# Polysketch attention and a top-2 router in one kernel: the head's order, TensorE's sketch sums and the last stores changed

## The chip, the core and the metric

The kernel runs on one core of a Trainium2 chip. Its engines are TensorE (PE; PEld is its weight load), VectorE (DVE), ScalarE (ACT), GpSimd (POOL) and SyncE (SP), which here only issues transfers. Each engine works through its own instructions in order and waits on semaphores. The metric is the device time of one execution in microseconds (us); less is better. Before the change the median of three runs is 347.21 us (346.69 to 347.39).

## What is computed

Inputs: q, k, v of 4 batches, 4 heads, 1088 tokens, head size 32; two sketch matrices S1, S2 (8 x 32, float64, read as words and split by the kernel); gate and noise weights (128 x 8), noise (4352 x 8), and w1 (128 x 1024), w2 (1024 x 128) of 8 experts.

```python
def phi(x):
    a = np.einsum('rd,bhsd->bhsr', S1, x)
    b = np.einsum('rd,bhsd->bhsr', S2, x)
    return np.einsum('bhsi,bhsj->bhsij', a, b).reshape(*x.shape[:-1], r * r)
q_p, k_p = (phi(q), phi(k))
kv = np.einsum('bhsf,bhsd->bhfd', k_p, v)
z = np.sum(k_p, axis=2)
num = np.einsum('bhsf,bhfd->bhsd', q_p, kv)
den = np.einsum('bhsf,bhf->bhs', q_p, z)[..., None] + 1e-06
# x = num / den, heads side by side: 4352 tokens of 128
noisy_logits = x @ w_gate + np.log1p(np.exp(x @ w_noise)) * noise
# the two best experts of each token, softmax weights top2_w over the two
h = np.maximum(x[mask] @ w1[e], 0.0)
out[mask] += top2_w[mask, k, None] * (h @ w2[e])
```

## The kernel before, in words

**Planner.** Nothing is issued in the order of the source. `add` gives a `Plan` a job: engine or choice of engines, a cost in us, the tiles it reads and writes, and `prio`. `Plan.order` is a list scheduler: among the jobs that can start within 0.3 us of the earliest it takes the least `prio`. So a changed cost or priority can move instructions on every engine, far from where it stands. Tile tags have a number of buffers; a job that opens a tile waits for the oldest user.

**Head, batch 0.** `decode_job` makes the sketch matrix `sk` on VectorE and TensorE, in a high and a low part (index c). `turned` transposes loaded keys (`kT`) or queries (`qT`) on VectorE. `features` multiplies them by `sk`, both parts side by side in a bank (L606); it evicts the low part to `lo` (ACT or DVE, L322), adds it to the high part on VectorE (`ab`, L614) and forms the products (`phk`, `phq`, L628). Keys of batch 0 come in tiles 0-1, 2-5, 6-7 and the half tile 8 (`C`). `keys_values` copies the values into `vaug`, sums keys x values on TensorE (L669), evicts them (`kvT`), folds in identity and gate weights (`wg`, L690), and evicts that as `kvw` in two halves. `queries` transposes the query sketches (L717, `pT`), makes numerators, denominators and gate logits in one matmul (L728), then on VectorE divisors and gates (`den`, `lh`, `lg`), on ACT or VectorE `x`. Two early sketches, of the rest of the queries of batch 0 and of the first keys of batch 1, have `early` set: they use the `acc` banks and stand between numerators and router. While TensorE would be idle in the head, `idle` puts warming matmuls of zeros there (`hp<-zb`).

**Router.** `router` computes noisy logits (VectorE, ACT, GpSimd), picks two experts, counts tokens per expert by matmuls of the mask `mk` with a triangle (L934, L937), works out each row's place (`to`), weighs the tokens (`xg`), and scatters them with GpSimd's indirect transfers to `xs` in DRAM (L809). The first half of batch 0 is router 0, the rest of it router 1, then batches 1 to 3. `clear` fills `xs` from `pad` ahead of the scatters.

**Experts.** `block` handles 128 or 256 rows of an expert: rows to `bT`, two matmul layers (L1108 into `hp`, relu on ACT, L1123 into `acc`), `y`, and a scatter into `pairs`. Blocks 0 to 3 take their rows by a one-hot matmul (`o`, L1047, L1050, L1054 and `turn`, L1060), blocks 4 to 7 fetch `xb` by GpSimd and turn it on TensorE (L1084), later ones fetch by SP and turn it on VectorE (L1096). The one-hot of the last of four token columns is made by two ACT operations.

**GpSimd's head.** Constants in a list by priority: `pads` (`pad`), `limits` (`reach`, `capt`), `numbers` (`pid`), the copies of the noise, and a choice of the value copies.

**End.** `sums` adds the two pairs of each token and stores them. For the last tiles of batch 3 the last two experts' results are not scattered but put in place by one-hot matmuls in `totals` (L1255) and added (L1186). The pieces are tiles 4-5, the half tile, tiles 6-7, all stored by ACT.

Of the kernel before, what the change touches and what calls it, by code (L numbers as in the profile page):

```python
# [174 lines left out]
def kernel(  # L175
# [27 lines left out]
    C = 8  # L203
# [58 lines left out]
    tag("lo", 2, [P, 4, 2 * R * H])  # L262
    tag("ab", 2, [P, 4 * H, 2, R])
# [54 lines left out]
    def copy(e, o, i):  # L318
        if e == "POOL":
            G.tensor_copy(o, i)  # L320
        else:
            paces.append(A.copy(o, i) if e == "ACT" else V.tensor_copy(o, i))  # L322

# [111 lines left out]
    def pool_job(cost, prio, emit, w, r=()):  # L435
        add("POOL", cost, lambda e: emit(), r=r, w=w, prio=prio)

    def constants():
# [51 lines left out]
        pool_job(1.2, 13, pads, ["pad"])  # L490
# [6 lines left out]
        pool_job(0.5, 14, lambda: limits(0, 1), [("limits", 0)], ["base"])  # L497
# [11 lines left out]
        pool_job(2.4, 15, numbers, ["pid"])  # L509
        pool_job(3.0, 16, lambda: limits(1, NW + 1), [("limits", 1)], ["base"])  # L510
# [84 lines left out]
    def features(jobs, prio, after=(), first=None, early=None):  # L595
# [7 lines left out]
        def emit(e):  # L603
            for i, (xT, t, _) in enumerate(jobs):
                lhsT = xT.t[:, P * t:min(P * t + P, S)]
                T.matmul(ps.t[rows, 2 * W * i:2 * W * i + 2 * W], lhsT=lhsT,  # L606
                         rhs=sk[:].rearrange("p c h x -> p (c h x)"), start=True, stop=True)
        last = (add if early is None else plan.add)("PE", n * mm(128), emit, lat=0.15, r=["sk"] + [(xT, t) for xT, t, _ in jobs],
                   w=[ps], prio=prio if first is None else first, touch=[dst for _, _, dst in jobs], after=after if early is None else (early,))
        lo, ab = new("lo"), new("ab")  # L610
        gone = [] if early is None else [onehot["pos"], onehot["gm"]]
        x4 = lambda: ps.t[rows, 0:2 * W * n].rearrange("p (i c y) -> p i c y", i=n, c=2)
        add(EV, either(W * n), lambda e: copy(e, lo.t[rows, 0:n, :], x4()[:, :, 1, :]), r=[ps] + gone, w=[lo], prio=prio)
        add("DVE", vec(W * n), lambda e: V.tensor_tensor(  # L614
            out=ab.t[rows, 0:n * H, :, :].rearrange("p (i h) w r -> p i (h w r)", h=H),
            in0=x4()[:, :, 0, :], in1=lo.t[rows, 0:n, :], op=ALU.add), r=[ps, lo], w=[ab], prio=prio if early is None else 12.95 if jobs[0][2] is kv_of[0][1] else 13.2)
# [20 lines left out]
    behind_gates = []  # L637

    def keys_values(b, prio, head=False, after=(), early=None):
        kT, qT, pk, pq, va = new("kT"), new("qT"), new("phk"), new("phq"), new("vaug")  # L640
        kld, qld, vld = klds[b], qlds[b], vlds[b]
        for h in range(H):
            add(("ACT", "POOL") if head else "ACT", {"ACT": act(256), "POOL": 0.4} if head else act(256), lambda e, h=h: copy(e, va.t[:, 0:C, h, 0:DH], vld.t[:, h, 0:C, :]),
                r=["ones_v"] + [(vld, l) for l in range(4)], w=[(va, h)], prio=prio + 2.2, after=hold)
        add("ACT", act(128), lambda e: A.copy(va.t[0:HB, C, :, 0:DH], vld.t[0:HB, :, C, :]),
            r=["ones_v", (vld, 4), (vld, 5)], w=[(va, H)], prio=prio + (2.9 if head else 2.2), after=hold)
        for i, (c0, c1) in enumerate(((0, 2), (2, 6), (6, 8)) if head else ((0, 4), (4, 8))):
            if early is not None and i == 0:
                turned(kT, kld, c0, c1, 22, True)
                features([(kT, t, pk) for t in range(c0, c1)], prio + i + 1, after, 21.5, early)  # L650
                continue
            freed.append(turned(kT, kld, c0, c1, prio + i))
            features([(kT, t, pk) for t in range(c0, c1)], prio + i + 1, after)
        freed.append(turned(kT, kld, 8, 9, prio + 1))
# [38 lines left out]
        for l in range(2):  # L693
            add(EV, either(98), lambda e, l=l: copy(
                e, kvw.t[64 * l:64 * l + 64, :, YW * l:YW * l + YW],
                ps.t[64 * l:64 * l + 64, 0:2 * YW].rearrange("p (a y) -> p a y", a=2)),
                r=[ps, "kvw0"], w=[(kvw, l)], prio=prio + 3)
        turned(qT, qld, 4, 8, prio + 5)
        if head:
            def rest(early):  # L700
                behind_first.append(features([(qT, C, pq)], prio + 26, (), 913))
                features([(qT, t, pq) for t in range(4, 8)], prio + 26, (), prio + 11, early)
# [71 lines left out]
    APART = "rows of other waves, or of other tokens"  # L774
# [41 lines left out]
    def router(b, t0, n, w, x, lg, prio):  # L816
# [28 lines left out]
        actf(0.25, lambda: A.activation(out=t3("sp"), in_=t3("u"), func=AF.Ln, bias=1.0), ["u"], ["sp"])  # L845
# [136 lines left out]
        indexed = dve(0.2 + 2 * vec(16 * n), index, ["first", "row"], ["f2", "at", "to"], late)  # L982
# [492 lines left out]
```

## Time and profile before

| what | us |
|---|---|
| median of 3 runs | 347.21 |
| profiled execution, its own time | 347.08 |
| its span in the trace | 345.1 |
| TensorE busy | 336.2 |
| first expert matmul starts | 27.47 |
| last matmul of TensorE starts its group (L1255) | 337.50 |
| last sum on VectorE starts | 339.25 |
| last store's issue starts, on ACT | 341.04 |

The span is counted from the first instruction to the last; the run's time has about 2 us more around it. In a timeline each line gives start, duration, engine, source line, operation, the tile written <- the tiles read, shapes, the number of instructions merged into the line, and in brackets the idle time of the engine ahead of it and what ended that. A float32 matmul appears as two passes. In the chain of waits each piece is what the end of the execution depended on at that time. "SPq" and "ACTq" are an engine's sequencer issuing a transfer.

### The profile page before, as it was taken

What the parts mean: (1) busy time and instruction counts of PE and PEld (TensorE: products, weight loads), DVE (VectorE), ACT (ScalarE), POOL (GpSimd) and SP (SyncE); (2) the same over time, 40 slices, a digit from 0 to 9 for tenths busy, and PEclk for the clock granted to TensorE, in tenths of its full rate; (3) what the DMA queues carried; (4) which work ended last, traced back from release to release, by engine and by line L of the source; (5) the groups of instructions that cost most, each with busy time, mean ns of one, the idle gap of its engine ahead of it and who ended that gap; (6) DMA issues with size and microseconds to landing.
All of it is one profiled execution on the core that took longest, in us unless ns stands there. A gap on an engine that the chain in (4) does not pass through costs nothing.

```text
span 345.1 us, 7493 instructions
## 1 busy us (share of the span) xinstructions
PE 336.2 (97%) x2585; PEld 313.9 (91%) x2586; DVE 146.4 (42%) x547; ACT 136.4 (40%) x305; POOL 232.1 (67%) x385
## 2 busy tenths in 40 slices
PE   8999999999999999999999999999999999999992
PEld 3859999999999999999999999999999999999992
DVE  5889794877636688555862000020102000112101
ACT  2357542543531445323334333433334333434430
POOL 8854868896899857898968889878334433354410
PEclk9999999999999999999999999999999999999997
DMA  7999839144571376511353213365125211114421
GB/s 217 327 346 268 288 63 356 60 116 114 139 221 39 62 187 133 138 40 39 74 74 71 54 43 54 69 184 120 37 36 185 67 32 27 29 32 166 147 77 39
DMA packets 68922, 41.17 MB, mean 119 GB/s; under 512 B 49877, under 2 KB 61078, under 8 KB 68880
## 3 DMA queue, kind: packets, MB, share of 16 engines
q1 hardware_dynamic: 63360, 30.93, 35.1%
q0 software_dynamic: 4704, 9.15, 8.2%
q10 hardware_dynamic: 816, 0.58, 0.6%
q8 instruction: 21, 0.34, 0.4%
q14 instruction: 21, 0.17, 0.2%
HBM read 24.18 MB, written 16.65 MB: 118 GB/s over the span
## 4 chain that ended last, share of the span: by engine, by line
PE 95%; DVE 2%; ACT 1%; issue 1%; POOL 0%; DVEq 0%; ACTq 0%; POOLq 0%
PE acc L1123 37%; PE hp L1108 37%; PE bank L606 5%; PE bank L728 4%; PE bank L669 4%; PE bank L717 2%; PE hp L1435 1%; PE acc L669 1%; PE bank L1255 1%; PE turn L1060 1%; PE bank L690 0%; ACT o L1050 0%; PE bank L937 0%; DVE lg L747 0%; ACT o L1047 0%
## 5 line engine op out<-in xcount | busy, mean ns | idle before, releaser
L1123 PEld LDWEIGHTS acc<-w2s,h 128*128 128x128 f32 x1152 | 145.8, 192 | 4.6
L1123 PE MATMUL acc<-w2s,h 128*128 128x128 f32 x1152 | 149.8, 275 | 0.0
L1108 PE MATMUL hp<-bT,w1s 128*128 128x128 f32 (+1 forms) x768 | 147.3, 328 | 0.2 <-ACT bT L322 0.2
L1116 ACT ACTIVATE h<-hp 128x512 f32<-128x512 f32 x144 | 86.0, 597 | 123.2 <-PE hp L1108 122.9
L1108 PEld LDWEIGHTS hp<-bT,w1s 128*128 128x128 f32 x768 | 111.6, 191 | 6.4 <-ACT h L1116 0.5
L809 POOL DMA_INDIRECT pairs<-y,ix x66 | 65.1, 986 | 66.1 <-ACT y L322 55.9
L809 POOL DMA_INDIRECT xs<-xg,to x72 | 73.0, 1014 | 19.2 <-issue 9.1
L808 POOL MEMSET zb<- 128x400 bf16 (+1 forms) x142 | 63.1, 444 | 0.2 <-PE hp L1435 0.2
L1096 DVE STREAM_TRANSPOSE bT<-xb 128x256 f32<-128x256 f32 (+1 forms) x40 | 15.6, 390 | 101.9 <-PE hp L1108 89.8
L322 ACT COPY y<-acc 128x128 f32<-128x128 f32 (+1 forms) x48 | 15.3, 320 | 28.1 <-PE acc L1123 27.6
L1179 DVE TENSOR_TENSOR o<-pr 128x512 f32<-128x512 f32 (+2 forms) x13 | 6.7, 525 | 36.1 <-DMA pr<-pairs 36.1
L728 PE MATMUL bank<-kvw,pT 128*128 128x98 f32 x144 | 18.2, 274 | 0.0
L728 PEld LDWEIGHTS bank<-kvw,pT 128*128 128x128 f32 x144 | 17.4, 192 | 0.6 <-DVE kvw L322 0.3
L669 PE MATMUL bank<-phk,vaug 128*128 128x128 f32 (+1 forms) x108 | 13.1, 277 | 0.0
L322 ACT COPY lo<-bank 128x256 f32<-128x256 f32 (+3 forms) x20 | 6.5, 328 | 16.5 <-PE bank L606 16.5
L322 ACT COPY pT<-bank 128x512 f32<-128x512 f32 (+1 forms) x16 | 8.8, 559 | 10.6 <-PE bank L717 9.1
L669 PEld LDWEIGHTS bank<-phk,vaug 128*128 128x128 f32 (+1 forms) x108 | 12.5, 191 | 0.4
L614 DVE TENSOR_TENSOR ab<-bank,lo 128x256 f32<-128x256 f32 (+3 forms) x20 | 7.2, 360 | 12.5 <-ACT lo L322 12.4
L628 DVE TENSOR_TENSOR phk<-ab 128x512 f32<-128x512 f32 (+1 forms) x20 | 12.2, 629 | 0.4
L628 DVE TENSOR_TENSOR phq<-ab 128x512 f32<-128x512 f32 (+1 forms) x20 | 11.8, 628 | 0.2
L991 DVE TENSOR_TENSOR xg<-x,g 128x512 f32<-128x512 f32 (+1 forms) x16 | 11.2, 750 | 0.0
L1435 PE MATMUL hp<-zb 128*128 128x512 bf16 x29 | 9.5, 463 | 1.6 <-DVE zb L439 1.3
(177 smaller groups left out, 243.7 us busy)
## 6 DMA issues: line engine op xcount, KB each, us to landing
xs<-pad SPq DMA_DIRECT2D x9, 516.0 KB
w1s<-in_moe_w_dram SPq DMA_DIRECT2D x8, 512.0 KB
w2s<-in_moe_w_dram SPq DMA_DIRECT2D x8, 512.0 KB
pr<-pairs SPq DMA_DIRECT2D x7, 512.0 KB
xb<-xs SPq DMA_DIRECT2D x96, 32.0 KB
kq<-in_k_dram SPq DMA_DIRECT2D x4, 544.0 KB
kq<-in_q_dram SPq DMA_DIRECT2D x4, 544.0 KB
vld<-in_v_dram SPq DMA_DIRECT2D x14, 128.0 KB
```

The source lines that it names most:

```text
L322: paces.append(A.copy(o, i) if e == "ACT" else V.tensor_copy(o, i))
L606: T.matmul(ps.t[rows, 2 * W * i:2 * W * i + 2 * W], lhsT=lhsT, rhs=sk[:].rearrange("p c h x -> p (c h x)"), start=True, stop=True)
L628: V.tensor_tensor(out=jobs[i][2].t[rows, jobs[i][1]:jobs[m - 1][1] + 1, :, :].rearrange("p c h (i j) -> p (c h) i j", i=R), in0=factors(i, ...
L669: T.matmul(kvp.t[:, P * a:P * a + P], lhsT=va.t[0:K, t, hs, :].rearrange("p h d -> p (h d)"), rhs=pk.t[0:K, t, hs, :].rearrange("p h f -> ...
L728: T.matmul(ps2.t[:, c0:c0 + 2 * YW], lhsT=pT.t[:, P * (2 * i + a):P * (2 * i + a) + P], rhs=kvw.t[:, a, :], start=True, stop=True)
L808: G.memset(zb[:, 0:FIRST_SPACER if kind == "first" else SPACER], 0.0)
L809: ins = G.indirect_dma_start(**kw)
L1096: add("DVE", vec(P * n), lambda _: V.transpose(bT.t[:, 0:P * n], flat()), r=[xb], w=[bT], prio=TOP + u)
L1108: T.matmul(hp.t[:, P * n * i:P * n * (i + 1)], lhsT=w1s[:, e, P * (js * g + i):P * (js * g + i + 1)], rhs=bT.t[:, 0:P * n], start=True, st ...
L1116: paces.append(A.activation(out=h.t[:], in_=hp.t[:], func=AF.Relu))
L1123: T.matmul(acc.t[:, D * c:D * c + D], lhsT=h.t[:, P * (n * i + c):P * (n * i + c + 1)], rhs=w2s[:, e, j, :], start=(j == 0 and c == 0), st ...
L1435: ins = T.matmul(warm()[:], lhsT=zb[:, 0:P], rhs=zb[:], start=True, stop=True)
```

## The change

- Buffers: `lo` is gone, `ab` has four buffers; the low part is evicted into `ab` and the sum made in place.
- Head order: `kT` of tiles 0-1 is turned at priority -51 (ahead of `sk`, -50), the next ones at 0.5 and 0.9, the half tile at 1.9. The first keys of batch 1 are turned after both halves of `kvw`.
- `summed`: the two early sketches are made by two matmuls of 64 columns per tile that accumulate in the bank; ACT evicts the sum in one copy, behind the router's logarithm.
- `kvw` of the head: one half on ACT, one on VectorE, declared to have no dependency on each other.
- GpSimd: page numbers (`numbers`), `pads` and the first limits behind the value copies, in that order; the other limits one by one, the last ones behind the first router's row indices.
- One-hots: block 0 has all four columns on VectorE; the ACT costs of the others are 0.45 for the planner.
- End: one store for tiles 4-7 by ACT, the half tile's by SP ahead of it; loads of these tiles (and of tiles 0-3) in two; the half tile's matmuls first.

As built, the order of instructions differs from before in these places that bear on time. On SP the keys of batch 1 and the weights of experts 1 and 2 stand ahead of the first two clears (before, three clears stood ahead of these weights). On GpSimd the second router's gate step (`g`, 128x5) stands ahead of the four fetches of `xb` and not behind them. On VectorE the copies `starts` and `over` stand between `c` and `noisy` of the first router. On TensorE there are fewer warming matmuls, and sketches, numerators and blocks 2 to 20 are interleaved differently.

```diff
+    tag("ab", 4, [P, 4 * H, 2, R])
...
     def pool_job(cost, prio, emit, w, r=()):
-        add("POOL", cost, lambda e: emit(), r=r, w=w, prio=prio)
+        job = add("POOL", cost, lambda e: emit(), r=r, w=w, prio=prio)
+        if 11 < prio < 11.5:
+            behind_values.append(job)
+        if prio == 17:
+            behind_choices.append(job)
...
-        pool_job(1.2, 13, pads, ["pad"])
+        pool_job(1.2, 11.45, pads, ["pad"])
-        pool_job(0.5, 14, lambda: limits(0, 1), [("limits", 0)], ["base"])
+        pool_job(0.5, 11.47, lambda: limits(0, 1), [("limits", 0)], ["base"])
-        pool_job(2.4, 15, numbers, ["pid"])
-        pool_job(3.0, 16, lambda: limits(1, NW + 1), [("limits", 1)], ["base"])
+        pool_job(2.4, 11.4, numbers, ["pid"])
+        for w in range(1, NW + 1):
+            pool_job(0.5 if w < NW else 0.3, 16 if w < 4 else 17, lambda w=w: limits(w, w + 1), [("limits", 1)], ["base"])
...
+                if summed:
+                    for c in range(2):
+                        T.matmul(ps.t[rows, W * i:W * i + W], lhsT=lhsT, rhs=sk[:, c, :, :].rearrange("p h x -> p (h x)"),
+                                 start=(c == 0), stop=(c == 1))
+                    continue
...
-        lo, ab = new("lo"), new("ab")
+        ab = new("ab")
+        if summed:
+            add("ACT", act(W * n), lambda e: copy(e, ab.t[rows, 0:n * H, :, :].rearrange("p x w r -> p (x w r)"), ps.t[rows, 0:W * n]),
+                r=[ps], w=[ab], prio=prio if early is None else 12, after=() if early is None else (onehot["sp"],))
+        else:
+            add(EV, either(W * n), lambda e: copy(e, flat(), x4()[:, :, 1, :]), r=[ps], w=[ab], prio=prio)
+            add("DVE", vec(W * n), lambda e: V.tensor_tensor(out=flat(), in0=x4()[:, :, 0, :], in1=flat(), op=ALU.add), r=[ps], w=[ab],
+                prio=prio)
...
-                turned(kT, kld, c0, c1, 22, True)
-                features([(kT, t, pk) for t in range(c0, c1)], prio + i + 1, after, 21.5, early)
+                turned(kT, kld, c0, c1, 22, True).deps.update(folded_first)
+                features([(kT, t, pk) for t in range(c0, c1)], prio + i + 1, after, 21.5, early, True)
-            freed.append(turned(kT, kld, c0, c1, prio + i))
+            freed.append(turned(kT, kld, c0, c1, (-51, 0.5, 0.9)[i] if head else prio + i))
...
+                if head:
+                    apart(ins, "kvw")
+                    wrote(ins, "kvw")
+            done = add(("ACT", "DVE")[l] if head else EV, 0.25 if head else either(98), half, r=[ps, "kvw0"], w=[(kvw, l)], prio=prio + 3)
...
-                if c == 3:
+                if c == 3 and u:
...
+            n = 2 if b == B - 1 and c == 4 else c
+            for d in range(0, c, n):
...
-        for k, cols in enumerate(((0, 1), (4,), (2, 3))):
+        for k, cols in enumerate(((4,), (0, 1), (2, 3))):
...
-    pieces = part_of(B - 1, [(4, 2), (6, 2)], True)
-    sums(B - 1, [pieces[0], pieces[2], pieces[1]], NW, 902, ("ACT",))
+    pieces = part_of(B - 1, [(4, 4)], True)
+    sums(B - 1, [pieces[1], pieces[0]], NW, 902, ("SP", "ACT"))
```

## The prediction

> **What bounds the kernel now.** I read the page's engine shares first, then the table by stage, then the chain of waits for the head, then the timelines of single engines where the change acts.
>
> ```profile
> PE 336.2 (97%) x2585; PEld 313.9 (91%) x2586; DVE 146.4 (42%) x547; ACT 136.4 (40%) x305; POOL 232.1 (67%) x385
> ```
> ```profile
> 27.47:47.73 20.26, 20.26 (x179) 19.95 (x180) 17.24 (x76) 11.64 (x32) 14.64 (x21) 1.00 0.81 226
> 47.73:70.00 22.27, 22.27 (x205) 21.66 (x203) 15.38 (x50) 8.29 (x20) 18.85 (x28) 1.00 0.53 173
> 70.00:150.00 80.00, 79.76 (x676) 77.12 (x675) 54.02 (x203) 32.96 (x77) 65.66 (x95) 1.00 0.51 126
> 150.00:320.00 170.00, 170.00 (x1217) 160.63 (x1216) 35.92 (x131) 65.95 (x124) 109.46 (x157) 1.00 0.30 73
> ```
> The columns after the stretch are its length, then the busy time of PE, weight loads, DVE, ACT and POOL. From 27.47 us on TensorE has no gap worth naming (0.24 us in 70 to 150). Time can be won only ahead of 27.47, where the expert work begins, and after TensorE's last matmul; anywhere else it can only be lost. The head's chain:
>
> ```profile
> 9.50 0.60 PE bank L606 x4
> 10.10 1.79 PE acc L669 x16
> 11.89 0.89 PE bank L606 x8
> 12.78 2.42 PE acc L669 x20
> 15.21 0.59 PE bank L717 x4
> ...
> 16.90 1.15 PE bank L728 x8
> ...
> 26.99 0.26 ACT lo L322
> 27.25 0.17 ACT bT L322
> 27.43 0.04 issue
> 27.47 2.05 PE hp L1108 x16
> ```
> From 9.50 to 15.21 TensorE is unbroken, and at the end two ACT copies in a row hold the first expert matmul: one evicts an early sketch, the next bT. The tail:
>
> ```profile
> 339.25 0.42 DVE L1186 TENSOR_TENSOR o<-o,bank 128x256 f32<-128x256 f32 x1 [0.36 <-PE bank L1255]
> ```
> ```profile
> 338.70 0.65 ACTq L338 DMA_DIRECT2D out_dram<-o  x1
> ```
> ```profile
> 339.45 1.50 ACTq L338 DMA_DIRECT2D out_dram<-o  x1
> ```
> ```profile
> 341.04 0.70 ACTq L338 DMA_DIRECT2D out_dram<-o  x1
> ```
> The last sum is ready at 339.67, but its store is issued at 341.04, because ACT is still issuing the half tile's.
>
> **What the Trainium skill says.** "TensorE: Matmul & The Clock Gate", section "LDWEIGHTS": a weight load takes its columns over 1.2, whatever else, thus 107 ns for 128 columns. The trace agrees: passes of 128 and of 98 columns both come every 0.11 us (1.79 us for 16, 1.76 for 16). "DMA: Bandwidth & Descriptors", "Anatomy of one DMA": about 2.0 us of a DMA are fixed. Here GpSimd waits 1.97 us after its last scatter. Same page, "Issuing engines are not separate DMA queues": a second issuing engine saves only issue time; here that is just what the tail lacks. "GPSIMD Engine Reference", specifications: GpSimd shares its SBUF interface with VectorE, so times of GpSimd vary; its two value copies took 0.66 and 0.40 us (the tile view).
>
> **The change part by part.** Times are of the profiled execution before.
>
> 1. First keys turned before the sketch. VectorE is idle from 5.55 to 6.15, waiting for TensorE, then does sk and the 0.36 us turn in a row; TensorE starts at 6.85. The trace's landing records put the keys' last piece at 5.93, so the turn fills only part of the gap: turn 5.95 to 6.31, sk to 6.62, TensorE at 6.66, a gain of 0.19. Tiles 6 and 7 are also turned before the first sum, so their sketches follow the others at once instead of at 9.50. With ACT's copy at 7.40 the sums and products run some 0.35 us earlier, the last small turn by 8.85, and TensorE is through its key sketches at 9.1. The 10.10 row can then start when the values are copied. GpSimd's two copies began at 8.52, behind the pads (7.33 to 8.51); now four small limits stand there, 0.89 us by the rows at 17.25 to 18.14, so copies from 8.3 to 9.3. Start 9.35 instead of 10.10: 0.75 earlier. Later products (10.9, 11.85, 12.65 for tiles 5, 7, 8) stay ahead of TensorE, so its end moves from 15.20 to 14.45. If GpSimd's small ones take longer, as one at 11.88 did with 0.64, it is 9.7 and 0.4. I take 0.7.
>
> 2. kvw halves on two engines. ACT's half starts at 16.32, VectorE's at 16.58 behind it, TensorE at 16.90. Declared apart, both run at 16.32: 0.26 less. Numerators at 15.95.
>
> 3. Keys of batch 1 turned after both halves, before the small query turn: from about 15.9 on VectorE. In before they landed at 17.05 by the landing records, after a 516 KB clear (15.79); now they take its place, at about 15.8. Turn to 16.6, small turn to 16.85, the divisors due at 17.1. No cost; each us that the keys come after 16.1 would stand on the path.
>
> 4. Copies of starts and over move between c and noisy: two small VectorE instructions, 0.08 us apart at 17.04: plus 0.12.
>
> 5. Early sketches summed by TensorE: 16 matmuls of 64 columns for 8 of 128, two passes each, so 32 passes of 0.11, not 16: 1.78 us more on TensorE from 17.8, to 21.4. Counts are due at 23.8. It replaces warming matmuls: nothing. ACT's two copies of 0.37 stand after the logarithm, the second at 21.4 and done at 21.8; the exponent behind it is due at 22.5: nothing. Were 64 columns dearer, at 0.15 a pass, it would be 0.3. Two 0.42 sums leave VectorE.
>
> 6. First one-hot wholly on VectorE, sketches' copies no longer ahead of bT. pos at 24.90 moves by 0.7 + 0.26 - 0.12 = 0.84 to 24.06. Four one-hots of 0.27 (1.62 for six) end at 25.4, the gathers at 25.8, ACT has done its pair by 25.35, bT 25.9, first expert matmul 26.2. Against 27.47: 1.25 us in all for the head.
>
> 7. GpSimd and SP. Page numbers and pads now follow the values: pads ready at 15.0 instead of 8.5, noise copies 15.5 to 17.8 (before 17.04), first needed at 20.6. The first two clears stand behind the weights of experts 1 and 2, so about 24.5 by the 3 us a pair takes; the first scatter needs them at 28.5. SP's queue keeps the weights moving: w1, w2 earlier, batch 1's values some 1.5 us earlier. Nothing on the path.
>
> 8. Scatters and the first fetches. VectorE reaches row at 26.2 (27.62 before), so scatters start at 28.5 (29.88) and end at 41.05 (42.45); landed 43.0. Now the second gate step stands before the four fetches on GpSimd, an added wait: behind it are the fetches, for which TensorE waits in order. It needs ACT's exponent, 45.61 before, 4.9 after the last numerators (40.67). In TensorE's new order these are done after 56 passes of experts and gathers and 38 more of the second router, 10.5 us after 26.2, so at 36.7; VectorE then has two rounds of divisors and gates of 1.05 before the 4.9 counted from the last round's end, less its own 1.1: the exponent at 42.6 to 42.8, the fetch at 43.3, landed 2.57 later (44.41 to 46.98 by the landing records), 45.9. TensorE asks for it at 26.2 + 20.26 - 0.44 (four sketch passes moved behind it) = 46.0. Cost nothing, 0.3 if any of this slips; before, there was 0.9 of slack (46.98 against 47.88).
>
> 9. Order of TensorE, VectorE and ACT from 28 to 100 differs because the planner sorts anew. Counts of matmuls after the start are equal, and I find no operand that is late by more than 0.2 through the first 20 us. Bounds: a gain of 0.2 (the gap in 70 to 150), a loss of 1.
>
> 10. Tail. The last tiles' matmuls keep their ten passes, the last sum still ends at 339.67. One store of 256 KB on ACT is issued at 339.72 instead of 341.04: 1.32 less. It moves twice the bytes with longer lines; 128 KB took about 0.6 us in the DMA view, so 0 to 0.6 more, I take 0.35. SP's half tile goes at 338.3, ahead. Net 0.95 (0.6 to 1.3). Splitting the loads adds VectorE instructions of 0.43 where it idles 10 us.
>
> Sum: 1.25 + 0.95 = 2.2 us. Span 345.1 becomes 342.9; the profiled execution took 347.08, so 344.9; the median of 347.21 is 0.13 above it, so 345.0.
>
> **Rivals.**
> A. The fetches hold TensorE. The head is shorter but block 4 waits at 46.0 for rows, a transfer chain that GpSimd's scatters pace at 1.57 us each. For: only 0.1 us of slack left. Against: the scatters start 1.4 earlier too. With scatters starting 0.6 later than I have it, 0.5 to 0.9 is lost: 345.8.
> B. The head does not move: value copies or keys of batch 1 late, so steps 1 and 3 give nothing; only 2, 6 and the tail remain, 0.26 - 0.12 + 0.41 + 0.95 = 1.5: 345.7. For: GpSimd's slow row at 11.88. Against: landing of a 516 KB clear at 15.79.
> C. Slower: the gate step on GpSimd. If the second router's exponent comes at 46.1 rather than 42.8 us, the fetch lands at 49.2 and TensorE stands 3.2 us at 46.0: 345.0 + 3.2 = 348.2. It decides from about 45.8 on (2.2 + 0.7 us lost). For: the exponent was at 45.61 before. Against: its numerators come 1.5 us earlier in TensorE's new order, besides the head's 1.25.
> D. The change is a wash: a few small stalls of step 9 eat the head, the one store is no faster: 347.2.
>
> **How the numbers follow.** What can be told from no change is 0.2%, 0.7 us: 346.5 to 347.9. Forecast 0.55, A 0.15, B 0.13, C 0.10, D 0.07. Faster 0.83, same 0.07, slower 0.10. The range runs from 344.1 (value copies at best, store at 1.3, the gap in 70 to 150 closed) to 346.9, leaving out C and about half of D.
>
> **What would show it.** TensorE's first expert matmul at 26.2 plus or minus 0.4, numerators near 16.0, VectorE's keys of batch 1 without a DMA wait, the transposes of block 4 with an idle time under 0.3, busy shares of 100% from 30 to 320, and one ACT store issued within 0.1 of the last sum. Wrong would be a first expert matmul after 27, TensorE waiting on xb, or more than 4.8 us from the store's issue to the span's end (4.06 before).

## The result, and the profile after

The changed kernel took 349.58 us (median of 8, 348.48 to 349.92), the kernel before beside it 347.03: a ratio of 1.0062, 95% interval 1.004 to 1.0083. The forecast was 345.0. Measured again in two other sets of runs (E5, E16 below), the same kernel took 347.70 and 347.71 us, ratios 1.0026 (1.0017 to 1.0034) and 1.0023 (1.0008 to 1.0039). So it is slower in all three; about 1.0 us of it comes back each time, and 1.5 us more belongs to the first measurement alone.

The profiled execution of the first measurement took 349.88 us, with a span of 348.2. Its table by stage, columns as before (stretch, length, then busy PE, weight loads, DVE, ACT, POOL):

```profile
27.47:47.73 20.26, 19.01 (x173) 18.67 (x171) 16.04 (x69) 10.21 (x27) 14.40 (x19) 1.00 0.76 228
47.73:70.00 22.27, 21.37 (x189) 20.62 (x190) 13.53 (x42) 7.75 (x20) 19.10 (x29) 1.00 0.59 185
70.00:150.00 80.00, 79.22 (x664) 75.73 (x664) 53.51 (x207) 31.70 (x76) 64.04 (x94) 1.00 0.52 125
150.00:320.00 170.00, 170.00 (x1215) 160.33 (x1214) 36.18 (x131) 66.54 (x125) 111.08 (x158) 1.00 0.31 69
```

TensorE was unbroken in all four stretches but for 0.24 us; now it stands still for 1.25, 0.90 and 0.78 us of the first three. Its timeline at the places that count:

```profile
26.32 0.38 PE L1135 MATMUL hp<-bT,w1s 128*128 128x128 f32 x1
```
```profile
43.55 0.71 PE L1150 MATMUL acc<-w2s,h 128*128 128x128 f32 x4 [1.04 <-ACT h L1143]
```
```profile
48.63 0.33 PE L1111 MATMUL turn<-ident,xb 128*128 128x128 f32 x1 [1.12 <-DMA xb<-xs]
```

The first expert matmul starts 1.15 us earlier than before (27.47), and then TensorE waits 1.04 us for ACT and 1.12 us for fetched rows. The chain of waits in this part (start, length, what):

```profile
31.71 3.24 POOL xs L833
...
41.38 0.97 POOL xs L833
42.35 3.25 issue
...
45.65 0.06 POOL g L968
...
46.47 2.12 DMA xb<-xs
48.59 0.04 issue
48.63 0.33 PE turn L1111
```

It runs over GpSimd: a scatter of 3.24 us, then the gate step `g`, then the fetch. Before, none of the first router's scatters was over 1.40 us, the gate step stood behind the fetches, and TensorE did not wait for the rows (GpSimd's and TensorE's timelines of before):

```profile
33.27 1.36 POOL L809 DMA_INDIRECT xs<-xg,to  x1 [0.17 <-issue]
34.63 0.34 POOL L808 MEMSET zb<- 128x280 bf16 x1
35.15 1.40 POOL L809 DMA_INDIRECT xs<-xg,to  x1 [0.17 <-issue]
...
44.41 2.22 POOL L338 DMA_DIRECT2D xb<-xs  x4 [1.97 <-DMA xs<-xg,to]
```
```profile
47.88 0.31 PE L1084 MATMUL turn<-ident,xb 128*128 128x128 f32 x1
```

So the fetch left at 44.41 before and at 46.47 now, while TensorE asks for the rows earlier than before. ACT's timeline says why the gate step came at 45.65:

```profile
39.13 0.37 ACT L321 COPY ab<-bank 128x256 f32<-128x256 f32 x1 [2.12 <-PE bank L618]
42.11 0.27 ACT L321 COPY y<-acc 128x128 f32<-128x128 f32 x1 [2.61 <-PE hp L1135]
42.27 0.24 ACT L868 ACTIVATE u<-u 128x40 f32<-128x40 f32 x1
```

The copy `y` needs a group of TensorE that ends at 39.83 in the records, but starts at 42.11. (`ab` ahead of it is late too, by 1.1 us: its group ends at 38.04 in the records.) Behind `y` in ACT's order stand `u`, from which the second router's exponent follows, and `h`, for which TensorE waits at 43.55. The tail, from the timelines of VectorE, SP and ACT:

```profile
341.61 0.87 DVE L1217 TENSOR_TENSOR o<-o,bank 128x256 f32<-128x256 f32 x2 [0.36 <-PE bank L1286]
```
```profile
341.27 0.59 SPq L338 DMA_DIRECT2D out_dram<-o  x1
```
```profile
342.51 0.65 ACTq L338 DMA_DIRECT2D out_dram<-o  x1
```

The one ACT store is issued right behind the last sum, as forecast, but the span ends 5.66 us later (4.02 before).

For all that follows I cut the span in three: up to the first expert matmul, from there to the start of the last group of placing matmuls (L1286, L1255 before), and the tail from there on. The last three rows are of one profiled execution each.

| | before | changed | E5 | E16 | E3 | E10 | E14 | E17 |
|---|---|---|---|---|---|---|---|---|
| median, us | 347.03 | 349.58 | 347.70 | 347.71 | 347.02 | 346.36 | 347.00 | 346.31 |
| kernel before beside it | | 347.03 | 346.69 | 346.71 | 346.64 | 346.67 | 346.71 | 346.78 |
| first expert matmul at | 27.47 | 26.32 | 26.85 | 26.95 | 27.25 | 27.38 | 26.59 | 26.67 |
| from there to the last block | 310.03 | 314.17 | 312.31 | 311.85 | 310.04 | 310.03 | 310.74 | 310.74 |
| tail | 7.56 | 7.67 | 7.77 | 7.64 | 7.05 | 6.73 | 7.96 | 7.06 |

The middle row is the finding: the kernel before needs 310.03 or 310.04 us in three profiles, whatever its tail; the changed one needs 1.8 to 2.3 us more, and 4.1 in the first measurement. The head's gain is paid back there. The columns don't add up to the medians: the profiled executions of E5 and E16 were the slowest of their sets (348.64 and 348.22), that of E3 was 0.5 us under its median (346.51). So E3's short tail row says less than its median.

### The profile page after: what moved, and what is told of

Read it like the earlier page. It is cut to its first block, busy times and chain, and to the rows that moved or that the text cites. A ratio compares the mean times of both kernels' runs of the same rounds, so it can differ in the third digit from the quotient of the medians.

```text
span 348.2 us, 7506 instructions
## 1 busy us (share of the span) xinstructions
PE 336.9 (97%) x2593; PEld 315.2 (91%) x2594; DVE 146.2 (42%) x548; ACT 135.3 (39%) x302; POOL 232.5 (67%) x385
## 4 chain that ended last, share of the span: by engine, by line
PE 88%; POOL 4%; DVE 3%; issue 2%; DMA 1%; ACT 0%; POOLq 0%; DVEq 0%
PE acc L1150 36%; PE hp L1135 34%; PE bank L618 4%; PE bank L752 4%; PE bank L688 4%; POOL xs L833 3%; PE bank L741 2%; PE hp L1466 1%; PE acc L688 1%; PE bank L1286 1%; POOL zb L832 1%; DMA xb<-xs 1%; DVE o L1081 1%; PE bank L709 0%; DVE o L1217 0%
## 5 line engine op out<-in xcount | busy, mean ns | idle before, releaser
L833 POOL DMA_INDIRECT xs<-xg,to x72 | 74.7, 1037 | 20.0 <-issue 8.6
L321 ACT COPY pT<-bank 128x512 f32<-128x512 f32 (+1 forms) x18 | 9.7, 550 | 9.9 <-PE bank L741 5.5
L321 ACT COPY ab<-bank 128x256 f32<-128x256 f32 (+3 forms) x19 | 6.1, 325 | 17.1 <-PE bank L618 12.5
L741 PE MATMUL bank<-ident,phq 128*128 128x128 f32 x72 | 10.9, 278 | 0.0
L630 DVE TENSOR_TENSOR ab<-bank,ab 128x256 f32<-128x256 f32 (+3 forms) x20 | 7.6, 381 | 7.2 <-issue 3.2
```

What stands on the lines that cost most here:

```text
L741: T.transpose(ps.t[:, c0:c0 + P], pq.t[:, t + i, 2 * a:2 * a + 2, :].rearrange("p h f -> p (h f)"), ident[:])
L833: ins = G.indirect_dma_start(**kw)
```

## The experiments

Times are medians of sets of runs beside the kernel before; every other number is from that kernel's own profile. Waits of TensorE are the idle times of its timeline (counted from weight load to weight load, as some of the expectations do, they are 0.1 us longer).

**E1: the half tile's store by ACT, all else as changed.**

```diff
-    sums(B - 1, [pieces[1], pieces[0]], NW, 902, ("SP", "ACT"))
+    sums(B - 1, [pieces[1], pieces[0]], NW, 902, ("ACT",))
```

> The changed kernel with one edit: the half tile's last store is issued by ACT, as before the change, not by SP; the big store stays one. Nothing else on any engine moves, so the rest is a second look at the changed kernel. Theory S (SP ends late: after its store SP reads the flag, branches and starts its closing waits only at 345.6): SP is done early, and the closing waits pass as the stores land, so the time from the big store's issue to the end falls from 5.7 us to about 5.0 and the median from 349.6 to about 348.9. Theory B (the bytes: the 256 KB store lands 3.1 us after its issue, and nothing else counts): still 5.5 to 5.7 us and about 349.5. For 37 to 49 us: if the late y copy of ACT (idle 2.6 us before it) and TensorE's waits of 1.04 and 1.12 us belong to the kernel they come again within 0.3 us; if they were of that one execution, y starts by 40.2, both waits are under 0.3 us and the profiled span is about 2 us shorter than 348.

Measured: 347.18 (before 346.64; 1.0015, 1.0008 to 1.0022). From the big store's issue to the end 4.94 us, as theory S has it. And the late copy did not come again; ACT's timeline of E1:

```profile
39.95 0.27 ACT L321 COPY y<-acc 128x128 f32<-128x128 f32 x1 [1.42 <-PE acc L1150]
...
43.54 0.21 ACT L931 ACTIVATE g<-g 128x5 f32<-128x5 f32 x1 [0.64 <-DVE g L930]
```

`y` starts as soon as its group ends, the wait at 43.5 is gone, and of the wait for rows 0.56 us stays. That left the question whether 2.4 us hung on one queue of the tail.

**E5 and E16: the changed kernel itself, twice more.**

> The changed kernel itself once more, nothing edited. E1, which differs from it only in the queue of the half tile's store, took 347.2 us with the kernel before at 346.6, while the changed kernel had taken 349.6 with the kernel before at 347.0. Theory S (it is the store on SP at the end): 349.3 or more again, with TensorE's waits at 43 and 48 us as in E1 and the loss after 340. Theory O (the late y copy and what followed it came from the circumstances of that measurement, not from the kernel): 347.2 to 347.9, no y copy that is late by 2 us, one wait of 0.6 to 1.1 us on the fetched rows near 47.

> The changed kernel itself, a third time. If the 349.6 of the first measurement was of its circumstances and 347.7 (E5) is the kernel: 347.4 to 348.0, TensorE's wait near 47 at 0.6 to 1.2 us and no y copy late by over 1 us. If the kernel falls into the late y copy in some sets of runs: 349 or more, with that copy late again.

Measured: 347.70 (347.2 to 348.64) and 347.71 (347.26 to 348.22). Theory O: the late copy is in none of the 18 profiles of the experiments; there `y` starts 0.04 us after its group. TensorE waits 1.05 and 0.62 us for the rows; here in E5:

```profile
47.80 0.33 PE L1111 MATMUL turn<-ident,xb 128*128 128x128 f32 x1 [1.05 <-DMA ix<-xs]
```

In the first profile the semaphore of the group before `y` rises at 42.09, 2.3 us after the records have the group end. Whether the signal was late or the records are displaced can't be told from one trace, and that it explains the 1.5 us of the other seven executions of that set is not shown, for they have no trace. E1 against E5 gives the store on SP its price: 0.5 us, not 2.4.

**E2: the gate step behind the fetches, as before the change.**

```diff
+        if w == 1:
+            behind_fetches.append(step)
...
+                for job in behind_fetches:
+                    job.deps.add(fetch)
```

> The changed kernel with one edit: on GpSimd the second router's first gate step goes behind the four fetches of rows, where it was before the change. Theory G (the gate step with its late exponent holds the fetches): the first fetch leaves at about 44.4 instead of 46.5, lands near 46.9, TensorE's wait for it (1.12 us) goes, and the median falls by 0.8 to 1.2 us to about 348.6. Theory R (the rows of the scatters arrive late anyway, or the next wait takes its place): fetch not before 45.5, the wait stays over 0.6 us, median 349.2 to 349.8. Neither touches the wait of 1.04 us at 43.5.

Measured: 347.13 (1.001, 1.0001 to 1.0019). The fetch leaves at 44.39, yet TensorE waits 0.85 us. Each theory is right by half: the gate step no longer holds the fetch, but now the rows of the last scatter do, landed at 43.74. The fetch leaves when it left before the change (44.41), for a TensorE that asks for the rows 1.6 us earlier (46.27, 47.88 before).

**E4: GpSimd's head order as before the change** (priorities of pads, page numbers and limits put back).

> The changed kernel with GpSimd's order in the head as before (pads ahead of the value copies, page numbers and limits behind the noise); SP's clears then leave early again, and TensorE's order is the same but for a few passes. Theory C (the two clears that the new order sends out at 31.65 us lengthen the third scatter from 1.4 to 3.2 us and with the other transfers make 37 to 49 us late): scatters are back to under 1.5 us, the last ends by 41.2, TensorE's waits at 43.5 and 48.6 shrink to under 0.5 us together, and the median falls by 1.5 us or more less the 0.5 us that the value copies cost in the head: about 348.5. Theory N (the clears do not matter; ACT's order does): the waits stay at 1.8 us or more in all and the head's loss comes on top: 349.6 to 350.3.

Measured: 347.36; the scatter of 3.23 us is still there, the last one starts at 41.71, the wait is 0.99 us. Theory C falls: in E4 no clear leaves between 12.47 and 34.96, so the one sent at 31.65 does not lengthen the scatter. Neither theory's time came, for both reckoned from 349.6.

**E6: those clears held behind the fetches; E8: the same on E7.**

```diff
-    for r in (2 * P, 3 * P):
-        clear(r, 52)
...
-    for r in (4 * P, 5 * P):
+    for r in (2 * P, 3 * P, 4 * P, 5 * P):
         later(DIRECT, lambda r=r: clear(r, 60 + r / P))
```

> The changed kernel with one move in SP's queue: the clears of rows 256 to 511 (two of 516 KB) go behind the first fetches instead of ahead of the weights at 31.7 us. In all kernels so far the fourth scatter starts at 35.0 to 35.8 and the last one lands at 43.5 to 43.8, whenever the first starts. Theory Q (the rows queue behind SP's transfers, 1.03 MB of them these clears, some 2.8 us at 370 GB/s): the last scatter lands by 42.0, the fetch leaves by 44.0, TensorE waits under 0.3 us for it, and the time is 0.5 to 1.0 us under that of the changed kernel beside it. Theory P (GpSimd's own pace sets it): last landing 43.4 or later, fetch at 44.4 or later, the wait stays over 0.5 us, same time within 0.3 us.

> E7 and besides the two clears held behind the fetches: the head of the change without what it lost. If theory Q holds, no wait of TensorE over 0.3 us from 26.4 to 100, and 0.7 to 1.0 us less than E7: 345.7 to 346.0, faster than both kernels. If theory P holds, as E7 within 0.3 us.

Measured: 354.55 and 355.50, 7 and 8 us worse than E5 and E7, which neither theory had. GpSimd's timeline of E6, then TensorE's, then TensorE's table by stage (stretch, length, busy PE, granted clock, DMA share, GB/s):

```profile
61.58 0.97 POOL L833 DMA_INDIRECT xs<-xg,to  x1 [4.69 <-ACT y L321]
```
```profile
79.48 0.22 PE L959 MATMUL bank<-mk,earlier 128*128 128x72 bf16 x1 [2.44 <-DVE mk L952]
```
```profile
82.90 3.46 PE L1135 MATMUL hp<-bT,w1s 128*128 128x128 f32 x16 [2.88 <-DVE bT L1123]
```
```profile
79.10:85.93 6.83, 3.57 (x24) 0.50 0.46 104
```

The second router's scatters write into the cleared rows and wait for the clears (one of the four, held and queued behind 2 MB of weights, landed at 60.76): they start at 61.58 instead of 50.51 (E5), and that reaches TensorE some 20 us later, as two waits of 5.3 us together. For 6.83 us from 79.10 the granted clock is 0.50 besides, and sixteen passes take 3.30 us (82.90 to 86.20) instead of 1.79: 1.5 us more. With the waits that makes 6.8 of the 6.9 us that E6 is behind E5. E8 has the same drop at 80.93; no other run has one before the last matmul. For the question asked, E6 still speaks: with 1.03 MB less ahead of them the last three scatters land 2.3 to 2.4 us after their start (4.3, 3.0 and 2.3 in E5), but the one of 3.23 us remains, the last starts at 41.35, and the wait is 0.60 us. So transfers are not what stretches a scatter.

**E9: VectorE's products apart.** GpSimd and VectorE in E16, the scatter that is stretched and what VectorE does meanwhile:

```profile
30.86 0.97 POOL L833 DMA_INDIRECT xs<-xg,to  x1 [0.17 <-issue]
31.82 0.35 POOL L832 MEMSET zb<- 128x280 bf16 x1
32.34 3.23 POOL L833 DMA_INDIRECT xs<-xg,to  x1 [0.17 <-issue]
```
```profile
31.91 1.62 DVE L643 TENSOR_TENSOR phq<-ab 64x256 f32<-64x256 f32 x3
33.45 1.28 DVE L643 TENSOR_TENSOR phk<-ab 128x512 f32<-128x512 f32 x2
35.15 0.16 DVE L767 TENSOR_SCALAR den<-bank 128x4 f32<-128x4 f32 x1 [0.42 <-PE bank L752]
```

Five products of two SBUF operands run without a break to 34.73; the scatter ends at 35.57, 0.84 us later, about its usual 0.97. All twelve profiles in which the third scatter takes over 2.3 us have this same 0.84 us. Before the change the products ran in two pieces, with an addition between them that waits for ACT, and the scatter got in there (33.27 to 34.63 above, 0.84 us after 33.79; VectorE of before):

```profile
32.51 1.28 DVE L628 TENSOR_TENSOR phq<-ab 128x512 f32<-128x512 f32 x2
33.83 0.22 DVE L614 TENSOR_TENSOR ab<-bank,lo 64x64 f32<-64x64 f32 x1
34.08 0.42 DVE L628 TENSOR_TENSOR phq<-ab 64x256 f32<-64x256 f32 x1
34.42 1.28 DVE L628 TENSOR_TENSOR phk<-ab 128x512 f32<-128x512 f32 x2
```

E9 puts three one-hots between the products:

```diff
+                if u == 3:
+                    one.deps.add(products[c])
+                    products[c + 1].deps.add(one)
```

> The changed kernel with VectorE's order alone edited between 30 and 34 us: three one-hots of block 3, which ran ahead of the products of the early sketches, now stand one before each of the first three 128x512 products, so that these no longer follow each other without a break. Theory V (GpSimd cannot begin a scatter while VectorE runs one tensor-tensor product straight after another; the third scatter of 3.24 us is 2.27 of such waiting and 0.97 of work): no scatter is over 1.7 us, the last starts by 40.5 instead of 41.4 to 41.9, the fetch leaves by 44.1, TensorE's wait for it falls from 0.65 to 1.14 us to under 0.3 us, and the median falls by 0.4 to 0.9 us from the 347.7 of E5. Theory D (the third scatter waits for the transfers, which free the fourth at 35.0 to 35.8 in every kernel): the fourth starts at 35.0 or later again, same wait, 347.5 to 347.9.

Measured: 347.70 (1.0024, 1.0013 to 1.0035), nothing gained; TensorE waits 0.90 us for the rows. The scatter of E9 and VectorE beside it:

```profile
31.85 2.39 POOL L835 DMA_INDIRECT xs<-xg,to  x1 [0.17 <-issue]
```
```profile
31.87 0.68 DVE L643 TENSOR_TENSOR phq<-ab 128x512 f32<-128x512 f32 x1
32.47 0.33 DVE L1083 TENSOR_SCALAR o<-place,pos,gm 128x128 f32<-128x128 f32 x1
32.73 0.67 DVE L643 TENSOR_TENSOR phk<-ab 128x512 f32<-128x512 f32 x1
34.11 0.16 DVE L769 TENSOR_SCALAR den<-bank 128x4 f32<-128x4 f32 x1 [0.71 <-PE bank L754]
```

The one-hot is no break: the scatter ends at 34.24, again 0.84 us after the last product (33.40), and is shorter only because one product moved out of the stretch. So V is right on who holds GpSimd. Theory D, which had the fourth scatter wait for transfers until 35.0, falls on that (it starts at 34.75, and at 34.50 in E14), though the time and the wait came out as D had them, for my remedy was half of one. The last scatter starts at 40.66, 1.2 us before E5's, and still the fetch leaves at 44.40: its rows land at 43.75, 3.1 us after the start.

Here the transfers come in. E11 and E12 (below) have the same scatters, the last at 40.58 and 40.49, and the same transfers in the same order on SP, only earlier or later: SP issues its second clear of this stretch at 33.48 in E11, 35.32 in E9 and 36.22 in E12, and the last rows land at 42.86, 43.75 and 44.76. That is the order of three executions, not an edit of the transfers.

**The rule for the fetch.** Over the 20 profiles one line fits each fetch to 0.01 us: it leaves 0.65 us after the last rows have landed, or 0.82 us after the gate step starts if that stands ahead of it and gives more.

| | before | changed | E5 | E2 | E9 | E11 | E14 |
|---|---|---|---|---|---|---|---|
| longest scatter, us | 1.40 | 3.24 | 3.23 | 2.97 | 2.39 | 2.38 | 1.39 |
| last scatter starts | 41.48 | 41.38 | 41.88 | 41.14 | 40.66 | 40.58 | 40.51 |
| its rows landed | 43.76 | 43.67 | 44.16 | 43.74 | 43.75 | 42.86 | 42.91 |
| gate step on GpSimd | behind | 45.65 | 44.27 | behind | 43.18 | behind | 43.65 |
| fetch leaves | 44.41 | 46.47 | 45.09 | 44.39 | 44.40 | 43.52 | 44.47 |

Three limits lie within about 1 us of each other: GpSimd's pace, the transfers ahead of the rows, the gate step. To relieve one shows the next. E11 alone has the fetch about as early as the forecast had it (43.3), and there TensorE does not wait for the rows.

**E13 to E15: expert 5's weights held behind the fetches** (1.05 MB less ahead of the rows), with the products apart (E13), alone (E14), and E13 with the tail of E10 (E15).

```diff
-    for e in range(2, E - 2):
+    for e in range(2, E - 3):
         load_w(e, 46 + e)
-    later(DIRECT, lambda: load_w(E - 2, 53), lambda: load_w(E - 1, 54))
+    later(DIRECT, lambda: load_w(E - 3, 52.5), lambda: load_w(E - 2, 53), lambda: load_w(E - 1, 54))
```

> E9 (products apart) and in SP's queue the 1.05 MB of expert 5's weights held behind the first fetches, with those of experts 6 and 7; the clears stay where the change put them. Theory VQ (two limits in a row, GpSimd's pace and the transfers ahead of the rows): the third scatter under 3 us, the last scatter starts by 40.7 and lands by 43.0, the fetch leaves at 43.7 to 44.0 (then the gate step's exponent holds it), TensorE's wait near 47 is under 0.4 us instead of 0.65 to 1.14, and 346.9 to 347.2 results, 0.5 to 0.8 less than the changed kernel beside it. Theory N (neither is the limit): wait over 0.6 us, within 0.3 us of the changed kernel.

> The changed kernel with expert 5's weights alone held. Theory VQ: GpSimd's third scatter of 3.2 us stays, the last one starts at 41.4 or later but lands 2.1 to 2.3 us after its start, fetch at 44.4 to 44.8, the wait near 47 stays at 0.5 to 0.9 us, and at most 0.3 us is gained. If the transfers alone were the limit: fetch before 44.0, wait under 0.3 us, 0.6 us or more gained.

> E13 with the tail of E10. E12 minus E9 gave -0.8 us for this tail: 346.1 to 346.4, so a little faster than the kernel before (346.65) and level with E10, unless the wait for rows at 122 us (0.34 in E9) grows by what is won at 47.

Measured: 347.46, 347.00 and 347.09. E13 does not show VQ: the products now began earlier and met the second scatter (2.58 us), the last one started at 41.45 again, and TensorE waited 0.86 us (0.52 in E15). E14 has no wait over 0.2 us near 47, and for a reason that I had not named. GpSimd, VectorE and TensorE of E14:

```profile
31.99 1.22 POOL L833 DMA_INDIRECT xs<-xg,to  x1 [0.16 <-issue]
```
```profile
30.75 1.62 DVE L643 TENSOR_TENSOR phq<-ab 64x256 f32<-64x256 f32 x3
32.30 0.15 DVE L1030 TENSOR_TENSOR lim<-stops,reach 128x8 f32<-128x8 f32 x1
32.48 0.17 DVE L1031 TENSOR_TENSOR over<-over,lim 128x8 f32<-128x8 f32 x1
32.56 1.29 DVE L643 TENSOR_TENSOR phk<-ab 128x512 f32<-128x512 f32 x2
```
```profile
46.31 1.14 PE L1150 MATMUL acc<-w2s,h 128*128 128x128 f32 x8
47.29 0.27 PE L1111 MATMUL turn<-ident,xb 128*128 128x128 f32 x1
```

By the sorting, two small steps that wait on each other fell between the products, which let the scatter through (1.22 us, its end 0.84 us after the product ahead of them): in the records `over` starts 0.03 us after `lim` ends, while in E9 the one-hot and the next product each start before the one ahead has ended; and eight passes of an expert moved ahead of the turn, so that TensorE asks for the rows at 47.2 instead of 46.3 (E1, E13). The fetch itself left at 44.47, held by the gate step. E14's 0.7 us against E16 come from these accidents of the order, from a shorter wait at 121 us (0.25, 0.54 in E16) and from a head that is 0.36 us shorter in its profile. Its last scatter starts about when E9's does and its rows land 0.8 us sooner, but so do E11's with no weights held; what the holding gave is not shown.

**E3, E7, E10: the tail.** E3 is the kernel before with the new tail alone. E7 is E2 with the old tail. E10 is the kernel before with three stores by ACT, the half tile's first:

```diff
-        for k, cols in enumerate(((0, 1), (4,), (2, 3))):
+        for k, cols in enumerate(((4,), (0, 1), (2, 3))):
...
-    sums(B - 1, [pieces[0], pieces[2], pieces[1]], NW, 902, ("ACT",))
+    sums(B - 1, [pieces[2], pieces[0], pieces[1]], NW, 902, ("ACT",))
```

> The kernel before with the new tail alone: last tiles summed and stored as one 256 KB store by ACT, the half tile's store by SP, the half tile's sums first. As predicted (a store issued 1.3 us earlier, 0.35 more for its bytes): 0.95 us faster, about 346.1. By what the changed kernel showed (3.1 us from issue to landing instead of 2.2, then closing waits that start 0.5 to 0.8 us later): between 0.2 faster and 0.3 slower, 346.8 to 347.3.

> E2 (the changed kernel with the gate step behind the fetches) and besides the tail as before: two stores of 128 KB on ACT, the half tile's between them. E3 minus the kernel before gave +0.4 us for the new tail. If that adds up, this takes 0.3 to 0.5 us less than E2, 346.6 to 346.8, level with the kernel before; if the new tail is no worse in this kernel, 347.1.

> The kernel before with its tail's order alone edited: the half tile's matmuls, sums and store go first and the two stores of 128 KB follow, all three by ACT. Theory I (what the tail lost before was ACT's issue of the half tile's store between the two): the last store is issued within 0.1 us of the last sum, 1.2 to 1.3 us earlier than before, lands 2.1 to 2.2 us later as before, and 345.3 to 345.6 results against 346.7. Theory J (the end is set by something else, as the closing waits or stragglers of the earlier stores): under 0.4 us gained.

Measured: E3 347.02 against 346.64 (1.0013, 1.0003 to 1.0024): the new tail is no gain but a small loss. E7 347.20: no better than E2, since another wait of 0.72 us came at 81 us with its order (and none near 47). E10 346.36 against 346.67 (0.9988, 0.9978 to 0.9999): a gain, of 0.3 us, as theory J had it, where 1.1 to 1.4 were expected by theory I. Its last stores, from ACT's timeline (three merged in one line):

```profile
338.19 2.46 ACTq L338 DMA_DIRECT2D out_dram<-o  x3
```

The last is issued at 339.64, 1.40 earlier than before, but its own issue takes 1.02 us right behind two others, it lands 2.71 us later (2.23 before), and the end is 4.50 after the issue (4.02). For the one store of 256 KB by the landing records: half of its queues are through 2.47 us after the issue, 0.35 later than with 128 KB, but the last is at 3.07 (2.23 before). And with a store on SP, SP takes its branch at the end only 0.28 us after ACT's issue and passes all its closing waits after the landing: from landing to their end 1.2 to 1.4 us, 0.9 in E1 and before.

**E11, E12, E17, E18: combinations.** E11 is E2 with E9's and E10's edits, E12 is E9 with E10's tail, E17 and E18 are E14 with the tails of E10 and E1.

> The changed head with the gate step behind the fetches (E2), the products apart (E9) and the tail of E10. The order after 50 us is sorted anew, so its small waits may differ. If V and I hold: scatters under 1.7 us, no wait of TensorE over 0.3 us up to 80 us, last store within 0.1 us of the last sum, and 345.0 to 345.8, faster than both kernels. If V fails, 346.0 to 346.3; if I fails too, 347.0.

> E9 with the tail of E10 in place of the one store, the gate step left where the change put it. E9 less 1.1 to 1.6 us if I holds (the new tail itself had cost 0.3 to 0.4): 345.5 to 346.0 if V holds too. The wait of 0.66 to 0.90 us for rows at 122 us, which the changed kernel has and E2 has not, should stay or grow by what the wait at 47 us gives back, since GpSimd's scatters of the third router set it: that would make it 345.9 to 346.4.

> E14 (expert 5's weights held) with the tail of E10 in place of the one store. If head and tail add up: E14 less 0.4 to 0.8 us, 346.2 to 346.6, level with E10 or a little under it and faster than both kernels. If the tail's gain is lost again, 346.9 to 347.1.

> E14 with the half tile's store by ACT, the big store left as one. E1 minus E5 gave -0.5 us: 346.4 to 346.7. Time from the big store's issue to the end 4.9 to 5.2 us instead of 5.9.

Measured: E11 347.15 and E12 346.91, neither faster than the kernel before. E11 frees the fetch (43.52) and has no wait near 47, but one of 0.68 us at 106 and one of 0.21 at 75 in its new order. E12's fetch leaves at 45.41, since its rows land late (above), and TensorE waits 1.40 us. E17 took 346.31 against 346.78 (0.9988, 0.9979 to 0.9997) and E18 346.47 (0.9986, 0.9978 to 0.9994): head and tail add up here. Both beat the kernel before by 0.3 to 0.5 us, which is not clear of E10's 0.3, and E10 leaves the head alone.

## Why the prediction was wrong, step by step

The forecast failed in the two steps that it had put at nothing, 8 (the rows for the first fetches) and 9 (the order behind them), and in step 10 (the tail), where the gain did not come. How much each was worth is told by counting, from the first expert matmul on, the time that TensorE's passes don't fill (each pass at its usual spacing in these traces, 0.11 us for 128 columns), against the kernel before. In us, gains positive:

| | forecast | first profile | E5 | E16 | E1 |
|---|---|---|---|---|---|
| head (steps 1 to 6) | 1.25 | 1.15 | 0.62 | 0.52 | 1.06 |
| from there to 50 us (step 8) | 0 | -2.57 | -1.20 | -0.77 | -0.71 |
| 50 to 80 us | 0 | 0.09 | 0.10 | 0.09 | 0.10 |
| 80 to 180 us (step 9) | 0 | -1.66 | -1.18 | -1.14 | -1.42 |
| tail (step 10) | 0.95 | -0.11 | -0.21 | -0.08 | 0.61 |
| span | 2.2 | -3.11 | -1.87 | -1.38 | -0.36 |

After 180 us nothing more is lost. E1 differs from the changed kernel in its tail.

Steps 1 to 6, the head: right. First expert matmul at 26.32, forecast 26.2; value sums at 9.26 (9.35), numerators at 16.14 (15.95), the keys of batch 1 turned at 16.02 without a wait for their transfer, early sketches hidden. In E5 and E16 one of GpSimd's copies of the values took 0.86 us instead of 0.40, the value sums came 0.5 us later, near step 1's worse case (9.7), and the matmul at 26.85 and 26.95, with about half the gain.

Step 7: right that its clears cost nothing on the path (E4), as far as the run tells. It did not say that two clears now leave among the scatters (31.65 and 35.10), where one did (33.24).

Step 8 failed: "the fetch at 43.3, landed 45.9 ... Cost nothing, 0.3 if any of this slips". It took the old scatters' 1.57 us each for the new ones. The scatters did start at 28.30 (28.5), but one took 3.24 us, because the head that came earlier and the early sketches that needed no sums brought five VectorE products together beside it. The prediction had named that GpSimd shares its SBUF interface with VectorE, but for the value copies, not for the scatters. The last scatter started at 41.38 instead of 40.08, 0.1 us from where it was before the change. Of the 1.97 us that GpSimd waited after its last scatter before the change, and that the prediction set beside a fixed cost of 2.0, 1.31 were the way to the landing and 0.65 came behind it.

Then the gate step: ACT's exponent was forecast at 42.6 to 42.8; it started at 43.54 in E1, at 45.35 in the first profile. By the rule for the fetch the rows alone would have let it leave at 44.39 (E1), 44.81 (E5), 45.04 (E16) and 44.32 (first profile); with the gate step it left at 44.66, 45.09, 45.20 and 46.47. TensorE asked at 46.3 (E1; forecast 46.0) and waited 0.6 to 1.1 us. So rival A, late rows, is most of it in the repeats, and rival C, the gate step, most of it in the first profile, though the exponent stayed short of the 45.8 from which C was to decide. They had 0.25 between them; what neither saw is that moving the head moves VectorE's work over GpSimd's.

Step 9 failed as well: "a gain of 0.2, a loss of 1". It was put at nothing in the sum, and between 80 and 180 us it cost 1.1 to 1.7 us, in the repeats as much as step 8. The largest wait there, 0.3 to 0.8 us at 123, is one in which VectorE's `bT` waits for fetched rows; the rest are short ones. Why the order leaves these was not settled; E2's order lacks the one at 123 and loses 0.4 us in this stretch.

Step 10: the store was issued 1.5 us earlier against TensorE's last block, as said and more, but "0 to 0.6 more, I take 0.35" for its bytes was 0.84 to its last queue, and the closing waits behind SP's branch, which the step left out, took 0.3 to 0.5 more. Another 0.3 us follows these waits in the first profile, but so it does in E1 and E7, whose stores all go by ACT, and these executions have 0.3 us less outside the span; it can't be laid to the store. "Net 0.95" was about zero: the tail is 7.67 against 7.56, and by E3's median it is 0.4 us of loss. Where E3 loses this its one trace, faster than its median, does not show.

Sum for the first profile: 1.15 gained in the head, 4.14 lost in the middle, 0.11 in the tail, 3.1 slower in the span (348.17 less 345.06), 2.8 in the two executions' own times. Of the 4.14 some 2 us go with the late copy of that measurement; the repeats have lost 1.8 to 2.3.

## What to carry to other kernels

Work that comes earlier does so only as far as the next resource that did not move: ask for every stage what else feeds the busy engine (here GpSimd's scatters), and whether that chain starts, paces and lands earlier too. A step that is put at nothing because its order is only sorted anew can cost as much as the one that was looked at (1.1 to 1.7 us here). When work is moved on VectorE, look at what GpSimd does at the same time, not only at VectorE's own readers. The last store paid for its slowest queue and for what the issuing engine still had to do after it; here an issue 1.5 us earlier was worth nothing.

## What the runs showed that was not expected

The Trainium skill, "SBUF — State Buffer", section "Who interferes with whom", says that a VectorE instruction with two SBUF inputs contends with a GpSimd instruction that reads SBUF, and infers that such an instruction leaves the writing of GpSimd's descriptors alone. The runs agree with the first: a scatter reads its row numbers from SBUF, and 0.97 us became 3.23 beside five products, 2.39 beside fewer (E9), and in both the scatter ended 0.84 us after the last product. Whether the reading was held or the writing of descriptors, which the page leaves free, they don't separate. The scatter was not held for one instruction but for the stretch; a one-hot between products did not let it in (E9, E13), two short steps that wait on each other did (E13, E14).

Taking 1.03 MB of clears out of a full queue (E6) cost 7 us, because the clears came back where the next scatters needed them: GpSimd did four other scatters first and stood still for 4.69 us, then ran from 61.58 to 78 us with no gap over 0.18 us and could not make up the 11 us by which these scatters began late.
